# Attention and spectral mixing on one core: value loads of four heads each, and the key cast ahead of the value casts

## The chip, the cores and the metric

The kernel runs on one core of a Trainium2 chip. The metric is the device time of one execution in microseconds, as the median of several runs. Before the change it is 437.87 us, the median of three runs (436.77 to 438.63).

## The reference

Two steps follow one another. The first is attention over 8 batches, 8 heads, 576 tokens and 64 elements per head, with a window of 128 tokens and a linear penalty on the distance:

```python
rel = pos[:, None] - pos[None, :]
mask = (rel >= 0) & (rel < 128)
scores = where(mask, q @ k.T / 8 - slope[h] * abs(rel), -1e9)
x = softmax(scores) @ v                      # then (8, 576, 512)
```

The second mixes along the sequence: a real FFT, 64 modes kept, a complex 512 x 512 weight for each mode, the inverse FFT, and a channel product with a ReLU:

```python
X = rfft(x, axis=1)[:, :64]
Yr, Yi = Xr @ w_r - Xi @ w_i, Xr @ w_i + Xi @ w_r     # for each mode
u = x + irfft(Yr + 1j * Yi, n=576)
out = u + maximum(u @ w_ch, 0)
```

Queries, keys and values are 9.4 MB each in float32. The two weight tensors are 67 MB each; they are cast to bfloat16 on their way into the core's memory.

## The kernel before

The attention works on 16 units; a unit is a batch and a group of four heads. A unit's query, key and value tiles arrive as float32 in the buffers `qr`, `kr` and `vr`, of which each has two halves that the units take in turn. VectorE casts them to bfloat16 (`cast`, L246 and L248 for values, L251 for keys and queries). TensorE transposes queries and keys (L263), ScalarE copies them out (L269), TensorE makes scores (L284, L297), ScalarE takes the exponential (L307), VectorE applies the table of penalties (`mask`, L318), TensorE multiplies by the values (`value`, L344) into the one output buffer `av`, and VectorE normalises (`norm`, L359 and L360). For every second unit TensorE forms the 64 modes (`spectrum`) and they are copied out (`channels`).

The order is written out by hand in the list `STAGE`: in each stage, step by step, a name, an argument and a lag; the step is done for the unit `stage - lag`. So in a stage the values of unit s are cast, the keys of unit s + 2 and the queries of unit s + 3. Nothing reorders the instructions of an engine afterwards.

`cast` ends with `self.load(w, u + 2)`: as soon as a half of a buffer has been cast, its next load is issued. All loads of queries and keys, and those of values for all but the last two units, are issued by SyncE, in the order of the casts (L232 queries and keys, L212 and L225 values). The values of the last two units are issued by GpSimd (L219, L225). The last 64 tokens of a unit, the tail, are a transfer of their own (L225).

DMAs issued by one engine take completion semaphores in turn, eight for SyncE and eight for GpSimd. A DMA waits until the one eight before it on that engine has landed.

GpSimd issues the weights. In each of the stages 1 to 13 it first copies one element of the keys that were cast in this stage (`gate`, L586), and then issues one weight transfer of 1 MB read, 512 KB written (L478), so that weights go out at the pace of the attention. From stage 12 on further weights go into the buffers that queries, keys and values no longer need. After the attention the weights stream through a ring of buffers (L512, L520), TensorE multiplies them with the modes (L983), and at the end the output is formed and written.

```python
if stage in AHEAD:
    nc.gpsimd.tensor_copy(gate[:1, :1], at.casted[stage + 2, "k"][:1, 0, 0, :1])
    load_w(AHEAD[stage], early)
```

Of the kernel before, what the change touches and what calls it, by code (L numbers as in the profile page):

```python
# [20 lines left out]
P = 128  # L21
# [6 lines left out]
FULL = 4  # L28
# [8 lines left out]

STAGE = (
    ("exp", 1, 0), ("score", 0, 0), ("exp", 0, 0), ("value", 0, 1), ("spectrum", None, 2),
    ("cast", "v", 0), ("score", 2, 0), ("channels", None, 2), ("transpose", "k", -1),  # L40
    ("cast", "k", -2), ("exp", 2, 0), ("norm", 0, 1), ("cast", "q", -3), ("score", 3, 0),
    ("mask", 1, 0), ("value", 1, 1), ("evacuate", "k", -1), ("mask", 0, 0), ("exp", 3, 0),
    ("transpose", "q", -2), ("evacuate", "q", -2), ("score", 1, -1), ("norm", 1, 1),
)
# [62 lines left out]
class _Attention:  # L107
# [93 lines left out]
    def load(self, w, u):  # L201
        nc = self.nc
        if u >= len(self.units):
            return
        b, g = self.units[u]
        hs = slice(4 * g, 4 * g + 4)
        if w == "v":
            t = self.raw[w][:, u % 2]
            sv = self.v[b, hs]
            if u < len(self.units) - 2:  # L210
                for h in range(4):
                    nc.sync.dma_start(  # L212
                        out=t[:, :2, h],
                        in_=sv[h, : FULL * P].rearrange("(r p j) d -> p r (j d)", r=2, j=2),
                    )
                queue = nc.sync
            else:
                for r in range(2):
                    nc.gpsimd.dma_start(  # L219
                        out=t[:, r],  # L220
                        in_=sv[:, 2 * r * P : 2 * (r + 1) * P].rearrange(
                            "h (p j) d -> p h (j d)", j=2),
                    )
                queue = nc.gpsimd
            queue.dma_start(  # L225
                out=t[64:96, 2],
                in_=sv[:, FULL * P :].rearrange("h (p j) d -> p h (j d)", j=2),
            )
        else:
            t = self.raw[w][:, u % 2]  # L230
            src = (self.q, self.k)["qk".index(w)][b, hs]
            nc.sync.dma_start(  # L232
                out=t.rearrange("p e j d -> p e (j d)"),
                in_=src.rearrange("(e h) (p j) d -> (h p) e (j d)", h=2, j=TPP),
            )
        self.loaded[w, u] = t
# [906 lines left out]
```

## Time and profile before

| | |
|---|---|
| median of three runs | 437.87 us |
| the profiled execution | 438.37 us |
| its span, first to last instruction | 436.6 us |
| mean granted TensorE clock | 0.86 |
| busy: PE, DVE, ACT, POOL | 73%, 44%, 37%, 22% |
| bytes that DMA moved, as written | 105.64 MB, mean 242 GB/s |
| read from HBM | 162.53 MB |
| end of the attention, last normalisation | 136.9 us |
| last multiply by weights | 402.6 us |

Engines are PE (TensorE), DVE (VectorE), ACT (ScalarE), POOL (GpSimd) and SP (SyncE); SPq is SyncE's queue of DMAs. `L212` is line 212 of the kernel. A share of the DMA engines over 1 means that packets overlapped on an engine. GB/s counts what was written: a weight is read as 4 bytes and written as 2, so a rate of 214 GB/s in the weights' part is twice that in reading. In a line of a timeline the first number is the start in us from the start of the span and the second the length. In a line of waits the numbers are us in total, times, and the longest.

### The profile page before, as it was taken

The numbers are of one execution on the slowest core, as the hardware profiler recorded it, in microseconds if no ns is written. First come the engines' busy times: TensorE is split into PE (matmuls) and PEld (weight loads), VectorE is DVE, ScalarE is ACT, GpSimd is POOL, SyncE is SP. The second block draws the span as 40 slices with busy tenths as digits, with TensorE's granted clock in tenths as the row PEclk, the third lists the DMA queues.
The fourth block names the chain that finished last, engine by engine and source line by source line (L and its number), as shares of the span: only waits on it lengthen the run. The fifth ranks groups of instructions, "written<-read, shape, count | busy, mean of one in ns | idle before, by whom it ended". The sixth has DMA issues, their size and how long they took to land.

```text
span 436.6 us, 7835 instructions
## 1 busy us (share of the span) xinstructions
PE 319.2 (73%) x3255; PEld 176.8 (40%) x3255; DVE 193.5 (44%) x335; ACT 163.7 (37%) x214; POOL 95.5 (22%) x183
## 2 busy tenths in 40 slices
PE   4689899979896635543442476898887999699893
PEld 3367577667665412111111133444434444233431
DVE  7789699887783301010000022343324342122784
ACT  6859799988681000000000012222233323101772
POOL 8701010103524101323212110101021110012600
PEclk9979899999899955555555579999999999989998
DMA  8999999999999999999999999999999999997697
GB/s 281 327 316 329 290 299 298 300 303 294 262 215 206 214 214 215 212 215 214 214 213 214 215 214 214 215 220 220 215 214 214 215 214 213 216 212 147 217 377 284
DMA packets 49988, 105.64 MB, mean 242 GB/s; under 512 B 4080, under 2 KB 21120, under 8 KB 49920
## 3 DMA queue, kind: packets, MB, share of 16 engines
q0 software_dynamic: 19456, 68.29, 77.7%
q1 hardware_dynamic: 30496, 36.86, 25.3%
q8 instruction: 25, 0.41, 0.4%
q14 instruction: 11, 0.09, 0.1%
HBM read 162.53 MB, written 9.44 MB: 394 GB/s over the span
## 4 chain that ended last, share of the span: by engine, by line
DMA 70%; PE 13%; DVE 7%; issue 5%; ACT 2%; SPq 1%; POOL 1%; DVEq 0%; POOLq 0%; ACTq 0%
DMA w<-in_moe_w_i_dram 38%; DMA wch<-in_moe_w_ch_dram 8%; DMA w<-in_moe_w_r_dram 8%; DMA qr<-in_q_dram 7%; PE av L344 2%; DMA qr<-in_moe_w_i_dram 2%; DMA kr<-in_k_dram 2%; DMA vr<-in_moe_w_r_dram 2%; DMA vr<-in_v_dram 2%; DVE vb L246 1%; DVE att L318 1%; PE my L736 1%; PE acc L983 1%; DVE x L360 1%; PE sc L284 1%
## 5 line engine op out<-in xcount | busy, mean ns | idle before, releaser
L983 PE MATMUL acc<-w,XC 128*32 128x512 bf16 x456 | 80.9, 480 | 71.2 <-DMA w<-in_moe_w_r_dram 34.0
L983 PEld LDWEIGHTS <-XC 128*32 128x32 bf16 x508 | 38.9, 148 | 111.9 <-issue 85.6
L307 ACT ACTIVATE att<-sc 128x1024 bf16<-128x1024 f32 x64 | 64.0, 1031 | 10.0 <-PE sc L297 10.0
L657 ACT CAST ZW<-zw 128x512 bf16<-128x512 f32 x8 | 4.7, 586 | 143.3 <-PE zw L655 143.3
L344 PE MATMUL av<-vb,att 128*128 128x132 bf16 (+1 forms) x576 | 38.7, 218 | 12.0 <-DVE x L360 7.4
L629 DVE TENSOR_SCALAR yq<-acc 128x512 bf16<-128x512 f32 x14 | 9.6, 687 | 82.9 <-PE acc L983 82.9
L344 PEld LDWEIGHTS <-att 128*128 128x128 bf16 x704 | 36.9, 99 | 17.4 <-DVE x L360 11.6
L742 ACT CAST XW<-my 128x512 bf16<-128x512 f32 x36 | 19.3, 589 | 51.6 <-PE my L701 51.6
L736 PE MATMUL my<-wch,xT 128*128 128x512 bf16 x144 | 34.7, 379 | 5.0 <-ACT x L776 2.7
L269 ACT COPY qkT<-tp 128x1152 bf16<-128x1152 bf16 x30 | 33.5, 1115 | 3.2 <-PE tp L263 2.4
L716 DVE COPY xT<-tr 128x1024 bf16<-128x1024 bf16 x16 | 19.5, 1220 | 24.9 <-PE tr L711 24.9
L512 POOL DMA_DIRECT2D w<-in_moe_w_i_dram x23 | 16.3, 709 | 64.3 <-PE acc L983 39.1
L512 POOL DMA_DIRECT2D w<-in_moe_w_r_dram x21 | 14.9, 711 | 64.6 <-PE acc L983 45.7
L777 DVE CAST x<-my 128x512 bf16<-128x512 f32 x17 | 11.8, 692 | 34.5 <-PE my L701 34.5
L297 PE MATMUL sc<-qkT 64*64 64x256 bf16 (+2 forms) x640 | 25.5, 267 | 2.1 <-ACT qkT L269 1.2
L360 DVE TENSOR_TENSOR x<-av,rec 128x640 bf16<-128x640 f32 x32 | 26.4, 824 | 1.1
L736 PEld LDWEIGHTS <-xT 128*128 128x128 bf16 x144 | 13.1, 97 | 24.3 <-issue 7.5
L297 PEld LDWEIGHTS <-qkT 64*64 64x64 bf16 x640 | 14.8, 110 | 20.0 <-issue 17.0
L246 DVE CAST vb<-vr 64x1024 bf16<-64x1024 f32 x32 | 22.6, 707 | 0.2
L284 PE MATMUL sc<-bias,ident 128*128 128x512 bf16 x64 | 21.5, 421 | 1.1 <-ACT att L307 1.1
L937 DVE TENSOR_TENSOR o<-yy,r 128x1024 f32<-128x1024 f32 (+1 forms) x21 | 20.7, 1018 | 2.5 <-ACT r L880 1.6
L318 DVE TENSOR_TENSOR att<-att,mask 128x1024 bf16<-128x1024 bf16 x32 | 20.5, 682 | 0.0
(153 smaller groups left out, 431.2 us busy)
## 6 DMA issues: line engine op xcount, KB each, us to landing
w<-in_moe_w_i_dram POOLq DMA_DIRECT2D x23, 1024.0 KB, 31.3
w<-in_moe_w_r_dram POOLq DMA_DIRECT2D x21, 1024.0 KB, 33.4
qr<-in_q_dram SPq DMA_DIRECT2D x16, 576.0 KB
kr<-in_k_dram SPq DMA_DIRECT2D x16, 576.0 KB
w<-in_moe_w_r_dram POOLq DMA_DIRECT2D x17, 512.0 KB, 19.1
vr<-in_v_dram SPq DMA_DIRECT2D x56, 128.0 KB
w<-in_moe_w_i_dram POOLq DMA_DIRECT2D x13, 512.0 KB, 24.0
out_dram<-o SPq DMA_DIRECT2D x8, 512.0 KB
```

The costliest lines, as they stand in the source:

```text
L246: nc.vector.tensor_copy(self.vb[u % 2][row, :, :, :, W * half : W * half + D], src[row, :2])
L269: (self.nc.vector.tensor_copy if u < 2 and w == "q" else self.nc.scalar.copy)(dst.rearrange("q h (p j) -> q h p j", j=TPP), tp.rearrange(" ...
L284: nc.tensor.matmul(sc[:, e], lhsT=self.ident, rhs=self.bias[:, hv].rearrange("p j n -> p (j n)"), start=True, stop=False, skip_group_check ...
L297: nc.tensor.matmul(sc[64 * half : 64 * half + 64, e, j * 256 + c0 : j * 256 + c0 + n], lhsT=qkT[row, 1, h, k0 + j : k0 + P : 2], rhs=qkT[r ...
L307: self.nc.scalar.activation(self.att[u % 2][:, kt * 8 * P : (kt + 1) * 8 * P], sc.rearrange("p e n -> p (e n)"), AF.Exp, scale=1.0 / math. ...
L318: nc.vector.tensor_tensor(out=rows, in0=rows, in1=self.table[:, heads], op=ALU.mult)
L344: nc.tensor.matmul(bank[:, qt * W : qt * W + rhs[j].shape[1]], lhsT=att[:, o : o + P], rhs=rhs[j], start=(n == 0 and j == 0), stop=(n == l ...
L360: nc.vector.tensor_tensor(out=self.x[:, b, :, cs].rearrange("p t (h d) -> p h t d", h=2), in0=tiles[:, :, :, :D], in1=rec.unsqueeze(-1).br ...
L512: nc.gpsimd.dma_start(out=into, in_=src)
L736: nc.tensor.matmul(mm, lhsT=xT, rhs=wch[:, dt], start=(dt == 0), stop=False, skip_group_check=True)
L937: nc.vector.tensor_tensor(out=whole(o, c), in0=part(yy, c), in1=whole(r, c), op=ALU.add)
L983: nc.tensor.matmul(into[32 * (m % 4) : 32 * (m % 4) + 32], lhsT=XC[:, c0 : c0 + 31 * NM + 1 : NM], rhs=wq[t][a], start=(ri == 0 and a == 0 ...
```

## The change

In `STAGE` the step `("cast", "k", -2)` takes the place of `("cast", "v", 0)` and the other way round, so in each stage VectorE casts keys first and then values; the loads that follow the casts are issued in that order as well. In `load`, the values of a unit come in two transfers, each of 256 token rows of all four heads, instead of four transfers, each of 512 token rows of one head. It is now one form for both queues; for the last two units, on GpSimd, nothing changes in it. The tail stays.

```diff
 STAGE = (
     ("exp", 1, 0), ("score", 0, 0), ("exp", 0, 0), ("value", 0, 1), ("spectrum", None, 2),
-    ("cast", "v", 0), ("score", 2, 0), ("channels", None, 2), ("transpose", "k", -1),
-    ("cast", "k", -2), ("exp", 2, 0), ("norm", 0, 1), ("cast", "q", -3), ("score", 3, 0),
+    ("cast", "k", -2), ("score", 2, 0), ("channels", None, 2), ("transpose", "k", -1),
+    ("cast", "v", 0), ("exp", 2, 0), ("norm", 0, 1), ("cast", "q", -3), ("score", 3, 0),
...
-            if u < len(self.units) - 2:
-                for h in range(4):
-                    nc.sync.dma_start(
-                        out=t[:, :2, h],
-                        in_=sv[h, : FULL * P].rearrange("(r p j) d -> p r (j d)", r=2, j=2),
-                    )
-                queue = nc.sync
-            else:
-                for r in range(2):
-                    nc.gpsimd.dma_start(
-                        out=t[:, r],
-                        in_=sv[:, 2 * r * P : 2 * (r + 1) * P].rearrange(
-                            "h (p j) d -> p h (j d)", j=2),
-                    )
-                queue = nc.gpsimd
+            queue = nc.sync if u < len(self.units) - 2 else nc.gpsimd
+            for r in range(2):
+                queue.dma_start(
+                    out=t[:, r],
+                    in_=sv[:, 2 * r * P : 2 * (r + 1) * P].rearrange("h (p j) d -> p h (j d)", j=2),
+                )
             queue.dma_start(
                 out=t[64:96, 2],
                 in_=sv[:, FULL * P :].rearrange("h (p j) d -> p h (j d)", j=2),
             )
```

## The prediction

> **What bounds the kernel now.** I read the page's slices first, then its queues and chain, then the trace by stretches of the attention part, then SyncE's and VectorE's timelines there.
>
> ```profile
> DMA  8999999999999999999999999999999999997697
> q0 software_dynamic: 19456, 68.29, 77.7%
> q1 hardware_dynamic: 30496, 36.86, 25.3%
> DMA 70%; PE 13%; DVE 7%; issue 5%; ACT 2%; SPq 1%; POOL 1%; DVEq 0%; POOLq 0%; ACTq 0%
> ```
>
> The DMA engines are at 9 tenths or more in every slice but the first and four at the end, the two queues' packets add to 103% of the 16 engines' span (packets overlap a little), and the chain is 70% DMA. So the kernel is one transfer stream to about 402 us (the last multiply by weights) plus some 34 us of output. An edit in the attention part pays only by what it changes in that stream: packets, time per packet, or holes.
>
> ```profile
> 24.94:45.74 20.80, 19.05 (x346) 14.26 (x344) 18.64 (x34) 17.52 (x19) 2.09 (x6) 0.94 1.09 315
> 45.74:78.79 33.05, 31.02 (x544) 23.13 (x544) 27.34 (x50) 29.18 (x34) 3.82 (x10) 0.95 1.07 298
> 78.79:109.00 30.21, 26.01 (x484) 20.38 (x483) 25.23 (x45) 26.27 (x30) 4.94 (x11) 1.00 1.08 300
> 140.00:400.00 260.00, 177.51 (x1086) 79.69 (x1085) 58.03 (x108) 35.59 (x64) 44.98 (x79) 0.80 1.06 214
> ```
>
> These are stretches cut where SyncE issues the values (columns: length, busy time of PE, PE's weight loads, DVE, ACT and POOL, clock, DMA share, GB/s written). Three stages from 24.94 to 45.74 take 6.9 us each at 315 GB/s; four from 78.79 to 109.00 take 7.55 us at 300. The DMA share is over 1 in both, so at most a small hole separates them. SyncE and VectorE show where one could be:
>
> ```profile
> SPq L212 <- DVE vt L248: 14.3, 7, 3.7
> SPq L212 <- DMA qr<-in_q_dram: 12.7, 8, 2.5
> ...
> 86.47 1.91 SPq L212 DMA_DIRECT2D vr<-in_v_dram  x4
> 88.49 2.08 SPq L225 DMA_DIRECT2D vr<-in_v_dram  x1
> 90.66 0.61 SPq L232 DMA_DIRECT2D kr<-in_k_dram  x1
> 91.37 0.42 SPq L232 DMA_DIRECT2D qr<-in_q_dram  x1
> ...
> 81.95 1.38 DVE L246 CAST vb<-vr 64x1024 bf16<-64x1024 f32 x2
> 83.25 0.41 DVE L248 CAST vt<-vr 32x512 bf16<-32x512 f32 x1
> 83.69 0.76 DVE L251 CAST k<-kr 128x1152 bf16<-128x1152 f32 x1
> 86.43 0.76 DVE L251 CAST q<-qr 128x1152 bf16<-128x1152 f32 x1 [1.00 <-DMA qr<-in_q_dram]
> ```
>
> The value cast frees its buffer at 83.33, yet SyncE issues the next values only at 86.47, just after a query load has landed (86.43). SyncE's program has eight completion semaphores in turn, and each DMA waits for the one eight before it. With seven DMAs a stage (four value heads, a tail, key, query) that is a query load little more than a stage old. Key and query queue behind: the key, cast by 84.45, is issued at 90.66. VectorE waits 1.00 us for a query here, and 6.5 us in six waits over the whole run.
>
> **The change, part by part.** The sum is made against the profiled execution, 438.37 us (span 436.6 and 1.8 around it), 0.5 above the median of 437.87.
>
> *Fewer transfers.* Two less in each of 14 units on SyncE, 28 in all. Bytes and rows stay: the rows are 512 bytes in memory both ways. In the trace's DMA packet records SyncE's queue has 16,128 packets of 512 bytes, which is 14 x (4 x 256 + 128); the 128 are the tails, already four heads to a transfer with 2 KB contiguous in the buffer, and they did not merge. So I expect 16,128 again. What goes is the completion packets, 16 per transfer: 28 x 16 x 10.6 ns (mean of their records) / 16 engines = 0.3 us of stream, all on the path. SyncE saves 28 x 0.48 us of issuing (1.91 / 4), 13.4 us, hidden: the engines are busy meanwhile.
>
> *The semaphore turn.* Five DMAs a stage instead of seven, so the DMA eight back is 1.6 stages old instead of 1.1. The wait for the query load (12.7 us over the run, about 3 us in each late stage) should go, and loads follow their casts: in the stage shown the key some 8 us sooner (82.7 against 90.66), the values some 2 to 3. What is late next is the transfer itself, so this is worth only the holes. Bounds: none (share over 1), or, if 45.74 to 109.00 ran as 24.94 to 45.74 does, 33.05 x (1 - 298/315) + 30.21 x (1 - 300/315) = 1.8 + 1.4 = 3.2 us. An inventory of the packets (27 ns for 512 bytes, 102 for a 2304-byte key or query row, 322 for a 4 KB weight row, 5% overlap) fills 4 to 104 us except about 1.5 us of holes. I take 1.2, nearer to the inventory, because it counts each packet.
>
> *Value packets.* 16,128 x 29.9 ns / 16 = 30.1 us of stream. Before, an engine reads two rows 64 KB apart for each partition; after, four rows 144 KB apart. No whole unit on SyncE shows that. Bounds: every packet at the commonest time, 27 ns, gives -2.9 us; every packet at 34.4 ns, their mean in the contended stretch 22 to 24 us, gives +4.5. I take 0: the tails have the new form already and no class of slow packets stands out.
>
> *Key cast ahead.* The same four casts, 0.76 + 1.38 + 0.41 us, stand together on VectorE. The value cast ends up to 0.76 later; its user L344 comes a stage later, about 6 us of cover. If that cover went, PE would lose at most 0.76 a stage, 16 x 0.76 = 12 us. If values land late, the wait now stands ahead of the normalisation (L359, L360), for which PE waits with its one output buffer `av`; now the query's stands behind it. Order on SyncE: key, values, tail, query; on GpSimd nothing moves. The gate copy (L586) that releases a weight transfer follows the key cast, so it opens about 1.8 us sooner, under the value casts. GpSimd's issue under a VectorE cast took 0.83 us (at 64.73) and 0.87 (109.26) against 0.53: 0.3 us more, hidden by the 4.6 to 9.1 us that it idles before each gate. Still one weight transfer a stage: 0.
>
> Sum: -0.3 - 1.2 = -1.5, so 436.9 for an execution like the profiled one, and 436.4 against the median. That is 0.34% less; about 0.5%, 2.2 us, is what a measurement of this kernel can tell from no change.
>
> **The rivals.**
>
> *The holes are all filled.* The late stages run at 315 GB/s: -0.3 - 3.2, perhaps with value packets at 28.5 ns (-1.4): 433.0 to 434.4. For it: VectorE's 6.5 us of waits and SyncE's 12.7. Against: a DMA share over 1 all along.
>
> *Slower: the four-head read is dearer.* Sixteen engines each walk four regions 144 KB apart instead of two, in L212's packets. At 34.4 ns: 436.4 + 4.5 = 440.9. It decides from where the 0.5% is lost: 1.5 + 2.2 = 3.7 us, a mean of 29.9 + 3.7 x 16 / 16.128 = 33.6 ns. For it: the mean was 34.4 and 36.8 ns in two short stretches (22 to 24, 10 to 12 us). Against: 11,000 of the packets take exactly 27 ns, which looks like the engine's own pace.
>
> *Slower: the values starve.* Key and weights go first, values land a little late, and VectorE stalls ahead of the normalisation. If a stall of 1.26 us (the longest for a query) came in each of 11 stages and opened an equal hole in the stream: +13.9 - 1.5, 450.3. It needs a landing over about two stages, 14 us; values landed in 5.8 to 12.4.
>
> *Each transfer's fixed cost is in the open.* Then two transfers less a stage would give at least SyncE's 0.48 us each: 437.87 - 13.4 = 424.5. Against: four value transfers are in flight together, and the engines are full meanwhile. The Trainium skill, "DMA: Bandwidth & Descriptors", section Rules for kernel authors, says to coalesce many small transfers into one large; with its fit of about 2 us fixed per DMA (section on the anatomy of one DMA), 28 fewer would by estimate be worth 56 us. The trace speaks against that, since those 2 us pass while the engines move other packets.
>
> **How the numbers follow.** Forecast (holes partly filled, packets the same) 0.45; holes all filled 0.30; dearer packets 0.20; starving 0.03; fixed cost 0.02. So faster 0.32, same 0.45, slower 0.23. The range runs from 433.0, the filled holes' far end, to 441.5, just over the dearer packets' 440.9. The forecast's own range is 435.7 (its 1.2 grown to 1.9, the rest of the 0.5%) to 438.0.
>
> **What would show it.** Right: SyncE's wait of L212 for a query load gone or under 3 us; SyncE's queue at about 30,050 packets (30,496 - 448); stages after 45.74 nearer 315 GB/s; VectorE's query waits below 6.5 us; the weights' part unchanged at 214 GB/s but starting 1 to 2 us sooner. Wrong: 512-byte packets with a mean over 33 ns, or merged into fewer, larger ones (a gain not counted here); VectorE waiting for `vr`; a DMA share under 1 before 110 us; any move of the time that arises after 140 us.

## The result, and the profile after

The changed kernel takes 440.22 us (median of 8 runs, 439.73 to 441.68), against 437.87 for the kernel before in the same comparison (8 runs). The ratio is 1.0055 with a 95% interval of 1.0034 to 1.0075: slower by 2.35 us, where 1.5 us faster was forecast. The profiled execution took 440.48 us, span 438.7. Line numbers of the changed kernel are 9 lower from L225 on (L246 is L237, L344 is L335, L478 is L469); all its value loads except the tails are L212, on SyncE and on GpSimd alike. Every ratio below leaves out executions that ran more than 1.5% longer than the quickest of the same kernel, among them one of 443.93 us in e6 and one of 711.3 us in e13.

The page of the changed kernel, in the lines that were shown of before:

```profile
DMA  8999999999999999999999999999999999997598
q0 software_dynamic: 19456, 68.29, 77.5%
q1 hardware_dynamic: 30048, 36.85, 25.1%
DMA 61%; PE 19%; DVE 8%; issue 5%; ACT 3%; POOL 2%; DVEq 0%; POOLq 0%; ACTq 0%
```

SyncE's queue lost exactly the 448 completion packets counted in the prediction, and the kernel is still bound by its transfers. The changed kernel in the same stretches:

```profile
24.94:45.74 20.80, 18.79 (x353) 14.01 (x350) 18.90 (x34) 17.71 (x19) 4.08 (x7) 0.95 1.08 310
45.74:78.79 33.05, 31.18 (x550) 23.53 (x546) 27.82 (x51) 29.28 (x33) 5.33 (x9) 0.95 1.08 308
78.79:109.00 30.21, 25.97 (x448) 20.14 (x445) 23.54 (x43) 24.61 (x28) 2.20 (x7) 0.94 1.07 303
140.00:400.00 260.00, 177.88 (x1063) 78.70 (x1060) 57.34 (x107) 35.02 (x64) 44.53 (x78) 0.78 1.06 215
```

Up to about 108 us this comes near the forecast: 308 for 298 GB/s and 303 for 300, though 310 for 315 in the first stretch. Counting each packet at its common time, the stream has done 1.0 us more work than before at 104 us and 1.1 more at 108. After 140 us nothing differs (215 against 214 GB/s), but the last multiply by weights is at 405.2 us instead of 402.6. So the loss lies between 108 and 140 us. Short stretches there, before:

```profile
108.00:110.00 2.00, 2.00 (x51) 1.85 (x49) 0.74 (x2) 1.90 (x3) 2.00 (x5) 1.00 1.10 319
110.00:112.00 2.00, 0.35 (x16) 0.09 (x4) 1.97 (x5) 2.00 (x3) 0.13 (x1) 1.00 1.11 337
112.00:114.00 2.00, 1.74 (x23) 1.74 (x24) 1.95 (x5) 0.85 (x1) 0.00 (x0) 0.72 1.06 230
```

and the same of the changed kernel:

```profile
108.00:110.00 2.00, 1.47 (x29) 0.88 (x23) 1.93 (x5) 1.81 (x2) 1.09 (x2) 1.00 0.54 149
110.00:112.00 2.00, 1.88 (x41) 1.78 (x45) 2.00 (x4) 1.20 (x3) 2.00 (x4) 1.00 0.79 227
112.00:114.00 2.00, 1.16 (x30) 0.89 (x23) 1.93 (x5) 2.00 (x3) 0.71 (x2) 1.00 0.73 160
```

The column before the last is the DMA share. It falls to 0.54, 0.79 and 0.73: a hole of about 2.3 us of work, which the kernel before does not have. A second, smaller loss of 1.3 us lies between 120 and 124 us, before and after:

```profile
120.00:124.00 4.00, 3.61 (x64) 2.48 (x61) 3.92 (x8) 3.40 (x5) 0.53 (x1) 1.00 1.07 218
120.00:124.00 4.00, 3.60 (x67) 2.31 (x58) 3.92 (x8) 3.52 (x4) 0.83 (x2) 1.00 0.95 151
```

This is the hand-over. SyncE has issued its last load, and what the stream gets next comes from GpSimd: the values of unit 14, and behind them the weights of stage 12. GpSimd's timeline of before:

```profile
106.18 1.89 POOL L219 DMA_DIRECT2D vr<-in_v_dram  x2 [5.65 <-DVE vb L246]
...
108.72 0.56 POOL L478 DMA_DIRECT2D w<-in_moe_w_r_dram  x1
```

and of the changed kernel:

```profile
108.91 1.53 POOL L212 DMA_DIRECT2D vr<-in_v_dram  x2 [9.58 <-DVE vb L237]
...
111.60 0.55 POOL L469 DMA_DIRECT2D w<-in_moe_w_r_dram  x1
```

Unit 14's values go into the half of `vr` that unit 12's value cast frees; GpSimd waits 9.58 us for that cast, and the weight, free to go once its keys are cast, stands behind it in program order: 111.60 instead of 108.72. Why the cast is late is seen on VectorE, before:

```profile
104.51 1.38 DVE L246 CAST vb<-vr 64x1024 bf16<-64x1024 f32 x2
106.25 0.76 DVE L251 CAST k<-kr 128x1152 bf16<-128x1152 f32 x1
```

and after:

```profile
105.47 0.75 DVE L242 CAST k<-kr 128x1152 bf16<-128x1152 f32 x1
107.23 1.39 DVE L237 CAST vb<-vr 64x1024 bf16<-64x1024 f32 x2 [1.01 <-DMA vr<-in_v_dram]
```

The stage comes 0.96 us later, the key takes its 0.75 first, and then the values themselves have not landed: 1.01 us of waiting. That makes 2.72 us. Before, SyncE issued unit 12's values at 94.09 and the key of the same stage behind them, at 98.35; now that key goes out at 91.77 and the values behind it at 94.97. The changed kernel's waits have this line for the whole run (us in total, times, longest):

```profile
DVE vb L237 <- DMA vr<-in_v_dram: 6.1, 4, 2.2
```

VectorE waited 6.5 us for queries before; now it waits for values, and for queries 1.1 us. SyncE's 12.7 us of waiting for a query load at L212 have shrunk to 0.2, as forecast:

```profile
SPq L212 <- DMA qr<-in_q_dram: 0.2, 1, 0.2
```

In their place its DMA instructions last longer (the changed kernel's SyncE timeline from the values on that SyncE issued at 86.47 before):

```profile
87.23 2.70 SPq L212 DMA_DIRECT2D vr<-in_v_dram  x2
90.02 0.78 SPq L216 DMA_DIRECT2D vr<-in_v_dram  x1
90.89 0.39 SPq L223 DMA_DIRECT2D qr<-in_q_dram  x1
91.77 3.12 SPq L223 DMA_DIRECT2D kr<-in_k_dram  x1
```

Two value transfers take 2.70 us here, where four took 1.91, and one key 3.12 instead of 0.61. Summed from 26 to 107 us, SyncE's DMA instructions last 52.5 us before and 70.5 after, with two fewer a stage. SyncE's last load is now unit 13's tail, at 104.17; before it was a key, at 106.04.

### The profile page after: what moved, and what is told of

Read it like the earlier page. It is cut to its first block, busy times and chain, and to the rows that moved or that the text cites. A ratio compares the mean times of both kernels' runs of the same rounds, so it can differ in the third digit from the quotient of the medians.

```text
span 438.7 us, 7780 instructions
## 1 busy us (share of the span) xinstructions
PE 322.1 (73%) x3255; PEld 176.6 (40%) x3255; DVE 193.9 (44%) x335; ACT 163.7 (37%) x214; POOL 99.2 (23%) x183
## 3 DMA queue, kind: packets, MB, share of 16 engines
q1 hardware_dynamic: 30048, 36.85, 25.1%
## 4 chain that ended last, share of the span: by engine, by line
DMA 61%; PE 19%; DVE 8%; issue 5%; ACT 3%; POOL 2%; DVEq 0%; POOLq 0%; ACTq 0%
DMA w<-in_moe_w_i_dram 31%; DMA wch<-in_moe_w_ch_dram 8%; DMA w<-in_moe_w_r_dram 8%; DMA vr<-in_v_dram 6%; DMA qr<-in_q_dram 5%; PE my L727 3%; PE acc L974 3%; PE av L335 2%; DMA vr<-in_moe_w_r_dram 2%; PE my L692 1%; PE tp L254 1%; DVE x L351 1%; DVE q L242 1%; DVE vb L237 1%; ACT XW L733 1%
## 5 line engine op out<-in xcount | busy, mean ns | idle before, releaser
L974 PE MATMUL acc<-w,XC 128*32 128x512 bf16 x456 | 82.8, 492 | 71.1 <-DMA w<-in_moe_w_r_dram 34.5
L335 PE MATMUL av<-vb,att 128*128 128x132 bf16 (+1 forms) x576 | 39.1, 219 | 11.3 <-DVE x L351 6.7
L335 PEld LDWEIGHTS <-att 128*128 128x128 bf16 x704 | 37.4, 100 | 16.9 <-DVE x L351 10.4
L237 DVE CAST vb<-vr 64x1024 bf16<-64x1024 f32 x32 | 22.7, 710 | 6.3 <-DMA vr<-in_v_dram 6.1
L577 POOL COPY gate<-k 1x1 bf16<-1x1 bf16 x13 | 5.5, 423 | 66.7 <-DVE k L242 66.7
```

The lines of the kernel that those rows point to most:

```text
L237: nc.vector.tensor_copy(self.vb[u % 2][row, :, :, :, W * half : W * half + D], src[row, :2])
L335: nc.tensor.matmul(bank[:, qt * W : qt * W + rhs[j].shape[1]], lhsT=att[:, o : o + P], rhs=rhs[j], start=(n == 0 and j == 0), stop=(n == l ...
L974: nc.tensor.matmul(into[32 * (m % 4) : 32 * (m % 4) + 32], lhsT=XC[:, c0 : c0 + 31 * NM + 1 : NM], rhs=wq[t][a], start=(ri == 0 and a == 0 ...
```

## The theories

A, the hand-over: unit 12's value cast comes late, GpSimd's next value load waits for it with the weights behind, and the stream runs dry because SyncE has nothing left; put down to the order of the casts. B, the four-head packets are dearer. C, GpSimd's weight issue falls under VectorE's casts and makes the weights' packets slow. D, a small loss in every stage. E, formed only after e9, is A with the order of SyncE's *loads* as what makes the cast late.

B falls on the traces: 16,128 packets of 512 bytes as before, mean 30.2 ns against 29.9, where 33.6 were needed. The kernel before was run beside each group: 437.77 us beside e1 to e4, 437.31 beside e6 to e9, 437.74 beside e10 and e11, 437.78 beside e12 and e13.

## The experiments: the two parts of the change

**e1**, the changed kernel again.

> The changed kernel as it is, for a second trace on the same chip as the next three. Theory A (the loss is a gap in the transfer stream where the attention hands over to the weights: GpSimd's load of unit 14's values, L212, waits for unit 12's value cast, and the weights stand behind it on GpSimd, while SyncE has no load left): 440.2 us, the DMA share falls below 0.8 between 107 and 114 us again, and the values again make VectorE wait in units 9 to 12. Theory B (512-byte packets dearer): 440.2 us, mean over 33 ns (the first trace had 30.2 against 29.9, which speaks against it already). Theory C (weight packets slow down because GpSimd issues them under the value casts): 440.2 us, and weight packets of over 0.8 us in several stages. The slow weight packets at 120 to 124 us (a second loss, 1.4 us) come again if they belong to the change, and not if they are chance.

Measured: 439.67 us (12 runs), ratio 1.0038 [1.0016, 1.0061]. The hole is there again but shallower (share 0.84 to 0.88 from 108 to 114 us where under 0.8 was expected, 0.91 from 120 to 124), unit 14's values at 108.63. The loss is real and some 2 us.

**e2**, the kernel before with the new order alone (four value transfers of one head).

```diff
-    ("cast", "v", 0), ...
-    ("cast", "k", -2), ...
+    ("cast", "k", -2), ...
+    ("cast", "v", 0), ...
```

> The STAGE of the changed kernel, values in four transfers of one head as before. Theory A: the value cast of unit 12 stands behind the key cast, so GpSimd's load comes at least 0.76 us later than before, but seven transfers a stage keep SyncE's queue as short as before, so values land sooner than in the changed kernel: 438 to 439.5 us, a smaller gap at about 108 us. Theory B: as before, 437.9. Theory C: 440.2, as the changed kernel, because the gate opens under the casts here too.

Measured: 439.77 us, ratio 1.0043 [1.0021, 1.0065], the whole loss and more than A had allowed (439.5 at most). VectorE's wait:

```profile
DVE vb L246 <- DMA vr<-in_v_dram: 6.6, 5, 2.1
```

The values are late with seven transfers a stage as with five, so the depth of SyncE's queue is not what starves them. Unit 14's values go out at 108.97, the share from 110 to 114 us is 0.83 to 0.86.

**e3**, two transfers alone: the changed kernel with the order of before (the edit of e2 undone).

> The STAGE of before, values in two transfers of four heads. Theory A: the key load is the last one on SyncE again and values are cast first, so no gap opens between 107 and 114 us, and the longer queue keeps the gain of about 1 us that the changed kernel had at 104 us: 436.5 to 438. If it is the longer queue and not the order that makes values late, VectorE waits for the values or keys here as well and the gap is there: 439 to 440. Theory B: 440.2 or more. Theory C: 437.9.

Measured: 437.92 us, ratio 1.0007 [0.9982, 1.0033]: no change that can be measured. Two of its stretches at the hand-over:

```profile
108.00:110.00 2.00, 2.00 (x45) 1.39 (x38) 1.97 (x5) 1.80 (x3) 2.00 (x4) 1.00 1.01 321
110.00:112.00 2.00, 1.84 (x44) 1.46 (x41) 1.96 (x4) 1.93 (x3) 1.49 (x3) 1.00 1.03 292
```

No hole like the changed kernel's (the share is 0.95 from 112 to 114 us); VectorE waits for queries and keys (4.0 and 2.0 us), never for `vr`, and unit 14's values go out at 107.28, 1.1 us later than before, which costs nothing that can be measured. In this trace (438.59 us) the stream is 0.6 us ahead of before at 104 us, has lost that by 116 and is 0.9 behind at 140: what is gained before the hand-over did not reach the end. The Trainium skill, "DMA: Bandwidth & Descriptors", section Rules for kernel authors, asks for few large transfers; the prediction's estimate of 56 us met a measured 0.15 us, inside the interval. The Trainium skill, "DMA: Bandwidth & Descriptors", section Anatomy of one DMA, makes the fit behind that estimate for DMAs that GpSimd issues, and the 28 are SyncE's.

## The experiments: where the order costs

**e7**, the kernel before with the new order from stage 10 on; **e6**, the changed kernel with the old order from stage 10 on.

```diff
-            for name, arg, lag in STAGE:
+            for name, arg, lag in (STAGE if stage < 10 else LATE_STAGE):
```

> The reverse: the kernel before (four transfers) with keys cast ahead of values from stage 10 on only. Theory A: 439.2 to 440.2 us, as with keys first everywhere, and the gap at 108 to 114 us. Theory D: 438 to 438.5 us, a quarter of the loss.

> The changed kernel (two transfers) with the order of before, values cast ahead of keys, from stage 10 on, and keys first before that. Theory A (hand-over: the order costs only where GpSimd's load of unit 14's values waits for unit 12's value cast): 437.2 to 438.2 us, and GpSimd issues unit 14's values before 107.5 us. Theory D (the order costs something in every stage, values starving VectorE from unit 9 on): 439 to 440 us, most of the loss stays.

Measured: e7 439.13 us, 1.0041 [1.0025, 1.0058], the whole loss from the last stages alone, which refutes D. Its trace (439.24 us) has a shallow hole only (share 0.90 from 112 to 114 us) and unit 14's values at 108.41, and there it is keys that VectorE waits for (5.1 us in three), not values. e6 438.98 us, 1.0028 [1.0010, 1.0045]: its trace (438.21 us) has no hole (share 1.04 to 1.08 from 108 to 114 us, unit 14's values at 106.46), but its executions spread from 436.6 to 440.3 and the median, where A had 437.2 to 438.2, regains only part.

**e10**, the kernel before with the new order from stage 12 on, and **e11**, the changed kernel with the old order from stage 12 on. SyncE's last loads are issued in stage 11, so these two change the order of casts at the hand-over and leave the loads' order. The diff is that of e7 and e6 with 12 for 10.

> The kernel before with the changed kernel's order of steps in stages 12 to 15 alone. Keys are loaded for the last time in stage 11's order of casts at SyncE, so here the order in which SyncE issues its loads is that of the kernel before; only the casts at the hand-over change places: in stage 12 unit 14's keys are cast ahead of unit 12's values. Theory A, cast order (unit 12's value cast comes later, so GpSimd issues unit 14's values later and the weights queued behind them too): those values issued at 107.5 to 109 us against 106.18 before, a hole of the stream between 108 and 114 us, and a time of 439 to 439.8, as with keys first from stage 10 on (439.13). Theory E, load order (what costs is that SyncE issues keys ahead of values, so that unit 13's tail instead of a key is its last load and unit 12's and 13's values land late): nothing in this kernel is late, the values issued within 0.7 us of 106.18 plus the key cast's 0.76, and 437.4 to 438.2, no change. Theory D, a loss in every stage: four stages of sixteen, 437.9 plus or minus 0.4.

> The changed kernel with the steps of stages 12 to 15 in the order of before (values cast ahead of keys); stages 0 to 11 are the changed kernel's, and so is the order in which SyncE issues its loads, all of which are issued by stage 11. Theory A, cast order: unit 12's value cast is the first of stage 12 again, GpSimd issues unit 14's values within 0.8 us of 106.5, no hole between 108 and 114 us, and 437.5 to 438.5. Theory E, load order: the values of units 12 and 13 still land late (unit 13's tail is SyncE's last load), VectorE still waits for vr, unit 14's values are issued at 107.5 or later, and 439.3 to 440.3, as the changed kernel (439.7 in its repetition). In between, with the values issued at 107 or so, both have a share.

Measured: e11 439.96 us, 1.0044 [1.0028, 1.0061]. Values are cast first in its stage 12, and they still wait:

```profile
108.17 1.39 DVE L245 CAST vb<-vr 64x1024 bf16<-64x1024 f32 x2 [1.89 <-DMA vr<-in_v_dram]
```

Unit 14's values go out at 109.86, and from 110 to 112 us the share is 0.51. So the cast order at the hand-over is not needed for the loss: A alone falls, E holds here. But e10, which leaves the load order, took 439.05 us, 1.0034 [1.0016, 1.0053], where E had 437.4 to 438.2. Its trace is of one of its quicker executions (437.98 us; the others reach 441.4) and shows no hole, with unit 14's values at 106.88, so that loss is measured but not seen in a trace. Either order seemed to be enough by itself, which the next two take apart over the whole attention.

**e12**, the changed kernel's casts (keys first) with the loads in the order of before; **e13**, the casts of before (values first) with the loads in the changed order.

```diff
+        if w == "k" and u > 2:
+            self.held = u + 2
+            return
         self.load(w, u + 2)
+        if w == "v" and u > 0:
+            self.load("k", self.held)
```

This is e12, at the end of `cast`; e13 is its mirror image, with the values' load held back until after the keys'.

> The changed kernel with its order of casts (keys, then values), but the load of the next keys is issued only after that of the next values, so SyncE's loads go out in the order of before (values, tail, key, query). Theory E (the order of the loads at SyncE makes values land late, the value cast of unit 12 wait, and with it unit 14's values and the weights behind them at GpSimd): VectorE's waits for vr under 2.5 us in all, unit 14's values issued by 107.3 us, DMA share at least 0.95 in 108 to 114 us, and 437.5 to 438.6. Theory A (the order of the casts by itself): 439.2 to 440.2 as the changed kernel, unit 14's values issued at 108 us or later. Both with a share: the values issued at 107 to 108 and 438.6 to 439.2; the kernel with keys first from stage 12 on alone had a cast order that cost 1.3 us, so this is well possible.

> The kernel with two transfers alone and the order of casts of before (values, then keys), but the load of the next values is issued only after that of the next keys, so SyncE's loads go out in the changed kernel's order (key, values, tail, query). Theory E: values land late as in the changed kernel, VectorE waits for vr 4 us or more in all, unit 14's values are issued at 108 us or later, a DMA share under 0.9 in a stretch of 108 to 114 us, and 439.2 to 440.2. Theory A: as two transfers alone, 437.5 to 438.5, no waits for vr over 1.5 us in all. In between, 438.5 to 439.2, both have a share.

Measured: e13 439.71 us, 1.0053 [1.0034, 1.0072], as E expected. Its wait:

```profile
DVE vb L237 <- DMA vr<-in_v_dram: 6.5, 7, 1.9
```

Unit 14's values go out at 108.59. The low share comes later than E had it, 0.76 from 118 to 120 us, and the stream is already 1.4 us behind at 104 (e12: 0.6), so these two lose a part ahead of the hand-over as well. e12 440.30 us, 1.0056 [1.0037, 1.0075], outside E's range and just over A's 440.2, for a reason that neither had. VectorE's wait and GpSimd's load in its trace:

```profile
DVE k L242 <- DMA kr<-in_k_dram: 7.9, 5, 3.3
```

```profile
110.64 1.54 POOL L212 DMA_DIRECT2D vr<-in_v_dram  x2 [10.35 <-DMA kr<-in_k_dram]
```

Now it is the key that lands late (3.00 us of waiting at 108.29), and since the keys are cast first, the value cast behind them, unit 14's values and the weights are late with it: share 0.54 from 110 to 112 us. Together:

| | loads: values first | loads: keys first |
|---|---|---|
| casts: values first | e3 437.92, 1.0007 [0.9982, 1.0033] | e13 439.71, 1.0053 [1.0034, 1.0072] |
| casts: keys first | e12 440.30, 1.0056 [1.0037, 1.0075] | changed kernel 440.22, 1.0055 [1.0034, 1.0075] |

Only one of the four keeps the time of before. The other three are not told apart: the changed kernel's repetition e1 has 1.0038. Of keys and values, the load that goes out later in a stage lands too late for its cast; the value cast of unit 12 must wait neither for its own load (right column) nor behind a key that does (e12), because GpSimd's next load hangs on it. With loads and casts both values first, what lands late is a key or query whose cast comes after the values', and GpSimd's load of unit 14's values does not wait for it.

## The experiments: closing the hole

**e4**, the changed kernel with one weight more at stage 11 and none at stage 13.

```diff
-    AHEAD = {stage: 1 for stage in range(1, 14)}
+    AHEAD = {**{stage: 1 for stage in range(1, 14)}, 11: 2, 13: 0}
```

> The changed kernel with the weight transfer of stage 13 issued in stage 11 already, two in that stage, ahead of unit 14's values on GpSimd; the same number of weights in the end. 2.4 us of transfer lie in the stream when the gap opens. Theory A: the gap at 108 to 114 us closes, 2.1 us come back: 437.5 to 438.5. If the hand-over is bound by the end of the attention (buffers come free at 122 and 128 us whatever is loaded before), the gap only moves to just before 128 us: 440. Theories B and C: 440.2.

Measured: 444.75 us, 1.0125 [1.0073, 1.0177]; four executions lie at 444.6 to 445.6 and two at 439.5 to 439.7, and the trace is of one of the slower four. The hole is filled (share 1.04 to 1.10 from 108 to 114 us), but the values of unit 13 land behind the extra weight, VectorE waits 6.82 us for them, and the stream runs dry where it had not (share, before the last column, 0.10):

```profile
120.00:124.00 4.00, 0.00 (x0) 0.00 (x0) 1.68 (x3) 0.07 (x1) 0.01 (x1) 0.79 0.10 25
```

**e8**, the changed kernel with the values of the last two units on SyncE too, so that no weight waits behind them; **e9**, the same edit to e3.

```diff
-            queue = nc.sync if u < len(self.units) - 2 else nc.gpsimd
+            queue = nc.sync
```

> The changed kernel with the values of units 14 and 15 issued by SyncE as well, so that the weights on GpSimd wait only for the key cast (gate) and no longer for the value cast. Theory A: the weight transfer of stage 12 starts at about 107 us instead of 111.5, the gap at 108 to 114 us closes: 437.5 to 438.7 us. A slower outcome under the same theory: the weights get ahead of unit 13's and 14's values in the shared engines, as they did with a weight transfer more in stage 11 (444.75 us), and the attention ends later: 441 to 445. Theory D: 439.7.

> The order of before, values in two transfers, and the values of units 14 and 15 issued by SyncE. Theory A: the hand-over of before had no gap at 108 us, so there is little to win: 437.0 to 438.2 us; if the weights get ahead of the last values, 441 to 445. Theory D says nothing of this kernel but 437.9.

Measured: e8 442.79 us, 1.0125 [1.0102, 1.0148]; e9 441.74 us, 1.0088 [1.0059, 1.0117]. The weights of stage 12 go out at 107.31 and 107.65 us and the hole is gone (e8: share 1.08 over 108 to 114). But the weights now run beside the last values instead of behind them, VectorE waits up to 6.1 and 8.4 us for `vr`, the last buffers come free at 135 us instead of 128, and in e8

```profile
130.00:140.00 10.00, 4.10 (x58) 2.98 (x57) 4.76 (x9) 2.81 (x4) 2.12 (x4) 0.84 0.49 104
```

The order of values and weights in one queue on GpSimd is worth more than the hole. The Trainium skill, "DMA: Bandwidth & Descriptors", section Issuing engines are not separate DMA queues, says that DMAs from different engines share the 16 DMA engines and interleave; e8 agrees, with 12.7 us of waits for values in seven where the changed kernel has 6.1 in four.

No version was faster than the kernel before.

## Why the prediction was wrong

- *Fewer transfers:* right in the count (30,048 packets, 16,128 of 512 bytes), and 0.3 us too small to be seen by itself.
- *The semaphore turn:* the wait at L212 went (12.7 to 0.2 us). It had been less than "about 3 us in each late stage": the line that the prediction shows has 12.7 us in eight waits, the longest 2.5. And "loads follow their casts" did not come true: the saved 13.4 us of issuing and the wait came back as longer DMA instructions, 70.5 us against 52.5. The key expected some 8 us sooner was issued 4.4 us sooner (86.29 for 90.66), the values expected 2 to 3 us sooner 0.8 later (87.23 for 86.47).
- *"So this is worth only the holes"*, 1.2 us: the term was about right up to 104 us (1.0 us with the 0.3 of the packets) and failed as a gain of the whole kernel. In e3's trace the 0.6 us gained was given back at the hand-over, and 1.0007 is what the part is worth. The step left out that what GpSimd loads after the hand-over waits for casts and freed buffers, whatever the stream has done before.
- *Value packets*, 0: right (30.2 against 29.9 ns).
- *Key cast ahead*, 0: the step that failed. "On GpSimd nothing moves" is true of the program's order, not of time. L219 on GpSimd waits for unit 12's value cast, in the one stage where GpSimd feeds the stream, with the weights behind it. The cast came 2.72 us later (107.23 for 104.51), the weight 2.88 later. The prediction allowed for up to 0.76 of that, the key's cast, and looked only at its user L344; the values that land late and the stage that starts late were put at nothing in the sum. e2 measures the order alone at 2.0 us, 1.0043.
- *The rivals:* the starving rival, with a chance of 0.03, named the right wait (VectorE for `vr`, 6.1 us in 4) at the wrong place: it was priced for PE behind the normalisation in 11 stages, and the attention ended as before (last normalisation at 136.5 against 136.9 us). In the changed kernel it costs at the hand-over, through GpSimd. The argument against it was a misreading: "5.8 to 12.4" is of GpSimd's transfers into `vr` alone, and the 12.4 is a weight; the view has no landing of SyncE's values. In the changed kernel one such load took about the 14 us that the rival asked for (the critical chain's line):

```profile
77.72 13.98 DMA vr<-in_v_dram
```

- *The other rivals:* holes filled (434.4 at most) and the fixed cost (424.5) are refuted by e3's 437.92, dearer packets by their mean.
- *The range:* 440.22 lies inside 433.0 to 441.5, but by luck. That end was set by the dearer packets, which did not come.
- *What would show it:* "a DMA share under 1 before 110 us" and "VectorE waiting for `vr`" were two of the signs of a wrong prediction, and both came. Of the signs of a right one all came but the last, an earlier start of the weights' part: they told of the early stages and not of the whole time.

Open: the second loss, 120 to 124 us. From 118 to 124 us the changed kernel has 12 weight packets of over 0.7 us (to 2.4, where the common one takes 0.32), together 1.1 us of all 16 engines; before has one. e1 has 11 and e2 16, but e3 has 9 and e10's quick execution 9 as well, so they are not the order's alone. C explains them by the casts beside the weight issues, yet in the changed kernel 8 of the 11 earlier weight issues fell under casts and none of these 8 was followed by such packets; no run here settles it. Open too are e10's loss, of which no trace shows the place, e6's spread, and why e13 and e12 are behind already at 104 us while the changed kernel is ahead.

## What to carry to other kernels

Where one engine's instruction order holds a load that waits for a buffer and, behind it, the loads that must keep the stream full, a change to the cast that frees that buffer is costed there, at the hand-over, however little it moves elsewhere. Of two loads issued in turn the later one lands late, so the load that something else hangs on goes first, and its cast goes first too; either order alone gave the whole loss here. And a full stream that is ahead in the middle need not be ahead at its end, if what follows is released by buffers and not by the stream; e3's one trace suggests that.

## What the runs showed of the hardware

A DMA instruction of SyncE is not a fixed cost: the same tail transfer lasted 0.57 us in the median before and 2.81 in the changed kernel, up to 4.17, and 7.36 in e4. SyncE waited less for completions (12.7 us at L212 became 0.2) and was held in the instructions instead (52.5 us became 70.5), so saved issues did not bring all loads forward. What holds it there is not shown.
